# Hash attention followed by a PReLU feed-forward: GpSimd only adds exponentials, reciprocals spread by the block turn, ones product joined to the v product, one PSUM pool for both stages with two feed-forward groups to a tile

## The chip, the cores and the metric

One core of one Trainium2 chip. Times are device microseconds of one execution, and a kernel's time is the median of its runs. Runs that agree within a fraction of a per cent are called fast; a kernel that ran only once has a run of unknown state, which is said where it matters. The granted clock is the share of its full rate that TensorE was given, as the trace records it. PSUM is the memory that takes TensorE's outputs; it is divided into banks, and a tile is a buffer of one or more of them.

## The reference

Attention in which a query sees only the keys of its own hash bucket (6 sign bits of a projection), then a feed-forward layer with a PReLU, all in float32.

```
batch, n_heads, seq, head_dim = (4, 8, 768, 64)
n_tokens, d_model, d_ff = (3072, 512, 2048)

q_bits = (einsum('bhsd,dk->bhsk', q, proj) > 0)          # k_bits likewise
mask   = q_bucket[:, :, :, None] == k_bucket[:, :, None, :]
scores = where(mask, scale * matmul(q, k.T), -1e9)
attn   = exp(scores - max) / (sum(exp(scores - max)) + 1e-9)
x      = matmul(attn, v)       # (B,H,S,D) -> (B*S, H*D)

h = x @ w_in
g = maximum(h, 0) + alpha * minimum(h, 0)
out = g @ w_out
```

## The kernel before

Work is cut into 16 head pairs, each of two units of 384 queries; a period in this text is one pair. In the loop, unit u computes scores in three parts of two key blocks, and beside that the unit before it, u-1, is finished: its exponentials summed (`add_first` on GpSimd, `add_last` on VectorE), multiplied by v (`attend`), summed over the keys by a product with ones, and divided. In between stand turns (transposes) and hash products of the next pair, and the conversion of the weights. TensorE's outputs go to small PSUM tiles: two `sc` tiles of two banks each, two `av`, two `mi`. The last are shared by the turns, the hash products and the sums.

```
    for u in range(UNITS + 1):
        ...
        if live:
            scores(u, 0)
            add_first(u, 0)
        if u > 0:
            add_last(u - 1)
            attend(u - 1, 0)
        if more:
            if g == 0:
                turn(pi + 1, "q", 0)
                turn(pi + 1, "q", 1)
            else:
                hash_bits(pi + 1, 0)
        if live:
            weight_parts(u)
            weight_sum(u)             # GpSimd
            scores(u, 1)
            add_first(u, 1)
        if u > 0:
            attend(u - 1, 1)
            ...
        if more:
            if g == 0:
                turn(pi + 1, "k", 0)
                turn(pi + 1, "k", 1)
            else:
                hash_bits(pi + 1, 1)
        if live:
            scores(u, 2)
        if u > 0:
            divide(u - 1)             # begins with the product with ones
        if live:
            weight_sign(u)
            ...
    attn.close()                      # frees SBUF and PSUM of the attention

    mpool = ctx.enter_context(tc.tile_pool(name="mlp", bufs=2))
    mpsum = ctx.enter_context(tc.tile_pool(name="mps", bufs=4, space=bass.MemoryType.PSUM))

    def ff1(b, ch, f):
        ps = mpsum.tile([P, CW], F32, name=f"h{b}_{ch}_{f}", tag="h", bufs=4)
        ...                           # four matmuls of 128x128 by 128x384, two passes each
        do(DVE.tensor_scalar(neg, ps, 0.0, alpha[:, f : f + 1], op0=ALU.min, op1=ALU.mult))
        ...
        do(DVE.scalar_tensor_tensor(g, ps, 0.0, neg, op0=ALU.max, op1=ALU.add))
```

## Time and profile before

| | before |
|---|---|
| time | 1087.3 us, median of 4 runs (1086.52 to 1089.06) |
| profiled span | 1082.9 us, granted clock 0.996 |
| attention, to the end of the last score product | 399.6 us |
| from there to the start of the third group of h | 19.75 us |
| from there to the end | 663.5 us |

The prediction below shows the page and the waits.

After the first wait TensorE stands for only 2.1 us in the second stage, in the verdict (a check of the inputs' magnitudes). One period of the attention, by the windows view (length, then busy us and instructions of each engine, clock, DMA share, GB/s):

```profile
252.00:276.69 24.69, 23.59 (x160) 10.37 (x156) 20.21 (x32) 15.96 (x27) 13.25 (x8) 1.00 0.33 91
```

TensorE is busy for 23.59 of 24.69 us.

### The profile page before, as it was taken

Reading aid. Unit: us, or ns where it says so; the run is one execution under the profiler, and the core shown is the slowest. Engines: PE = TensorE matmul, PEld = TensorE weight load, DVE = VectorE, ACT = ScalarE, POOL = GpSimd, SP = SyncE. Lnnn points to the kernel's source line nnn. Section 1 sums busy time; section 2 is a strip of 40 time slices with the busy share of each in tenths; the row PEclk is TensorE's granted clock in tenths of the full one; section 3 lists DMA queues with packets and bytes.
Section 4 is the critical chain, followed back from the end, with each engine's and each line's share of the span. In section 5 each row is a group of like instructions: output and inputs, shape, how many; then the busy total and the mean of one; then the engine's idle time right before and its main releaser. Section 6 shows DMA issues by size and latency. Waiting matters only on the chain.

```text
span 1082.9 us, 10697 instructions
## 1 busy us (share of the span) xinstructions
PE 1042.6 (96%) x4292; PEld 508.9 (47%) x4292; DVE 483.8 (45%) x795; ACT 271.1 (25%) x441; POOL 214.8 (20%) x144
## 2 busy tenths in 40 slices
PE   6999999999999998999999999999999999999997
PEld 3444444444444434544544544544544544554543
DVE  4887888878888794401411410410410420420410
ACT  6566666666656640000000000000000000000000
POOL 4455555455544560000000000000000000000000
PEclk9999999999999998999999999999999999999999
DMA  6333333333333200000000000000000000000000
GB/s 172 92 83 84 84 93 103 88 98 83 98 87 99 69 1 1 1 10 20 0 10 19 1 10 20 1 10 20 1 10 20 0 10 19 1 10 14 6 10 22
DMA packets 62843, 42.73 MB, mean 39 GB/s; under 512 B 51504, under 2 KB 55616, under 8 KB 62784
## 3 DMA queue, kind: packets, MB, share of 16 engines
q1 hardware_dynamic: 62784, 41.96, 13.7%
q8 instruction: 35, 0.57, 0.2%
q14 instruction: 24, 0.20, 0.1%
HBM read 35.66 MB, written 6.29 MB: 39 GB/s over the span
## 4 chain that ended last, share of the span: by engine, by line
PE 78%; DVE 17%; ACT 3%; issue 1%; DMA 0%; SPq 0%; POOL 0%; DVEq 0%; ACTq 0%
PE h L735 31%; PE z L748 30%; PE sc L603 7%; PE av L635 6%; DVE st L658 2%; DVE kb L588 2%; DVE accd L624 2%; DVE accd L625 2%; ACT pt L608 1%; PE sm L651 1%; PE tp_k L567 1%; PE tp_q L567 1%; DVE wr L549 1%; ACT qb L591 1%; DVE xT L660 1%
## 5 line engine op out<-in xcount | busy, mean ns | idle before, releaser
L735 PE MATMUL h<-xT,w_in 128*128 128x384 f32 x1024 | 333.4, 488 | 2.9 <-DVE xT L660 2.9
L748 PE MATMUL z<-w_out,g 128*128 128x512 f32 x768 | 330.9, 592 | 0.0
L740 DVE TENSOR_SCALAR neg<-h,alpha 128x384 f32<-128x384 f32 x128 | 79.1, 618 | 467.3 <-PE h L735 467.3
L735 PEld LDWEIGHTS h<-xT,w_in 128*128 128x128 f32 x1024 | 195.2, 191 | 141.3 <-issue 8.6
L748 PEld LDWEIGHTS z<-w_out,g 128*128 128x128 f32 x768 | 145.9, 190 | 182.0 <-issue 179.9
L753 ACT COPY o<-z 128x512 f32<-128x512 f32 x24 | 14.0, 585 | 663.2 <-PE z L748 663.2
L603 PE MATMUL sc<-qT,kT 64*128 64x384 f32 x768 | 155.5, 482 | 0.0
L608 ACT ACTIVATE pt<-sc 128x768 f32<-128x768 f32 x192 | 148.4, 808 | 21.7 <-PE sc L603 20.9
L635 PE MATMUL av<-pt,vn 128*64 128x385 f32 (+1 forms) x768 | 137.9, 494 | 0.0
L619 POOL TENSOR_TENSOR accp<-accp,pt 128x768 f32<-128x768 f32 x64 | 108.5, 1695 | 2.5
L635 PEld LDWEIGHTS av<-pt,vn 128*64 128x64 f32 x768 | 49.6, 136 | 80.4 <-issue 80.4
L603 PE MATMUL sc<-qb,kb 64*128 64x384 bf16 x384 | 64.1, 326 | 16.9 <-ACT pt L608 16.8
L603 PEld LDWEIGHTS sc<-qT,kT 64*128 64x128 f32 x768 | 69.1, 188 | 14.7 <-issue 14.4
L742 DVE SCALAR_TENSOR_TENSOR g<-h,neg 128x384 f32<-128x384 f32 x128 | 71.4, 558 | 4.4
L616 POOL TENSOR_TENSOR accp<-pt,pt 128x768 f32<-128x768 f32 x32 | 64.5, 2016 | 39.4 <-ACT pt L608 38.6
L603 PEld LDWEIGHTS <-kb 64*128 64x128 bf16 x384 | 24.1, 93 | 77.3 <-issue 61.1
L591 ACT ACTIVATE qb<-hs,bq 32x384 bf16<-32x384 f32 x64 | 36.6, 573 | 79.4 <-DVE kb L588 78.8
L624 DVE TENSOR_TENSOR accd<-pt,pt 128x768 f32<-128x768 f32 x32 | 54.7, 1710 | 0.0
L658 DVE COPY st<-rc 128x384 f32<-128x384 f32 x32 | 46.3, 1446 | 1.1
L655 DVE STREAM_TRANSPOSE st<-sm 128x384 f32<-128x384 f32 x32 | 18.6, 582 | 54.7 <-PE sm L651 54.7
L552 POOL TENSOR_TENSOR wr<-w_out,wr 128x512 f32<-128x512 f32 x16 | 20.6, 1285 | 76.3 <-DVE vs L641 42.0
L552 POOL TENSOR_TENSOR wr<-w_in,wr 128x512 f32<-128x512 f32 x16 | 20.5, 1282 | 72.3 <-DVE vs L641 41.5
(73 smaller groups left out, 467.5 us busy)
## 6 DMA issues: line engine op xcount, KB each, us to landing
raw<-in_moe_w_in_dram SPq DMA_DIRECT2D x16, 512.0 KB, 3.8
raw<-in_moe_w_out_dram SPq DMA_DIRECT2D x16, 512.0 KB, 3.6
qn<-in_q_dram SPq DMA_DIRECT2D x32, 192.0 KB, 3.3
kn<-in_k_dram SPq DMA_DIRECT2D x32, 192.0 KB, 3.2
vn<-in_v_dram SPq DMA_DIRECT2D x16, 384.0 KB, 3.2
out_dram<-o SPq DMA_DIRECT2D x24, 256.0 KB, 2.0
wh<-in_proj_dram SPq DMA_DIRECT2D x2, 1.5 KB, 2.5
alpha<-in_moe_alpha_dram SPq DMA_DIRECT2D x1, 8.0 KB, 1.9
```

The lines of the kernel that those rows point to most:

```text
L591: do(ACT.activation(bits["q", pi][D * s : D * s + 32, cols], ps[r], AF.Sign, bias=bq[r]))
L603: do(PE.matmul(sc[:, s, :CW], what["k", pi][r, ks], what["q", pi][r, qs], start=first, stop=not first,))
L608: do(ACT.activation(pt[:, :, :CW], sc[:, :, :CW], AF.Exp, scale=SCALE))
L616: do(POOL.tensor_tensor(accp[u], p[0], p[1], op=ALU.add))
L619: do(POOL.tensor_tensor(accp[u], accp[u], t, op=ALU.add))
L624: do(DVE.tensor_tensor(accd[u], p[0], p[1], op=ALU.add))
L635: do(PE.matmul(av[u][D * s : D * s + D, :w], nat["v", pi][:, s, kc * D : (kc + 1) * D], prob[u, kc][:, s, :w], start=(kc == 0), stop=(kc = ...
L658: do(DVE.tensor_copy(a.rearrange("p (n w) -> p n w", w=32), r.unsqueeze(2).to_broadcast([P, CW // 32, 32])))
L735: do(PE.matmul(ps, w[:, kk, o : o + P], xT[b][:, kk, ch * CW : (ch + 1) * CW], start=(kk == 0), stop=(kk == NK - 1),))
L740: do(DVE.tensor_scalar(neg, ps, 0.0, alpha[:, f : f + 1], op0=ALU.min, op1=ALU.mult))
L742: do(DVE.scalar_tensor_tensor(g, ps, 0.0, neg, op0=ALU.max, op1=ALU.add))
L748: do(PE.matmul(ps, gT[b, ch, f][:, t * P : (t + 1) * P], w_out[f // 4][:, f % 4], start=(f == 0), stop=(f == NF - 1),))
```

## The change

The intent, as I read it: VectorE and GpSimd contend for SBUF ports in the attention (a copy of 0.36 us takes 1.65 beside GpSimd, in the prediction's lines), and TensorE stands between the two stages. So GpSimd keeps only the adds of exponentials (the weight sum goes to VectorE); the copy that spreads the reciprocals goes, and the second 32x32 block transpose reads a broadcast operand instead; the product with ones follows the product with v directly, so that the array changes its tiling less often; and one PSUM pool serves both stages, so that the first two groups of h can run inside the last chunk's tail. For the last part the groups of h take the two `sc` tiles, two groups to a tile of two banks.

```
     def weight_sum(i):
-        do(POOL.tensor_tensor(wr[i], piece(i)[0], wr[i], op=ALU.add))
-    def weight_sign(i):
         lo, hi = halves(i)
+        do(DVE.tensor_tensor(wr[i], piece(i)[0], wr[i], op=ALU.add))
         do(DVE.scalar_tensor_tensor(...))                    # sign
 ...
+    def totals(u):
+        sums[u] = psum.tile([P, CW], F32, name=f"sm{u}", tag="mi")
+        for s in range(2):
+            do(PE.matmul(sums[u][D * s : D * s + D], ones, accd[u][:, s], start=True, stop=True))
 ...                                                          # in divide:
-        do(DVE.tensor_copy(a.rearrange("p (n w) -> p n w", w=32), r.unsqueeze(2).to_broadcast([P, CW // 32, 32])))
-        do(DVE.transpose(d, a))
+        do(DVE.transpose(d, r.unsqueeze(2).to_broadcast([P, CW // 32, 32])))
 ...                                                          # the loop
+        weight_parts(u)
         if more: ... turn q / hash half 0
-        if live:
-            weight_parts(u)
-            weight_sum(u)
         scores(u, 1)
         add_first(u, 1)
+        weight_sum(u)
         if u > 0:
             attend(u - 1, 1)
+            totals(u - 1)
         if more: ... turn k / hash half 1
         scores(u, 2)
         if u > 0:
             divide(u - 1)
-            weight_sign(u)
 ...
     def ff1(b, ch, f):
-        ps = mpsum.tile([P, CW], F32, name=f"h{b}_{ch}_{f}", tag="h", bufs=4)
+        if f % 2 == 0:
+            hs[b, ch] = psum.tile([P, 2, 512], F32, name=f"h{b}_{ch}_{f}", tag="sc")
+        ps = hs[b, ch][:, f % 2, :CW]
 ...
+    attend(last, 0)
+    ff1(0, 0, 0)
+    add_last(last)
+    attend(last, 1)
+    ff1(0, 0, 1)
+    totals(last)
+    divide(last)
+    attn.close()
```

Cut: nine instead of eight exponential buffers, smaller pools, the output z in the `av` tiles, the verdict in the `mi` tiles.

More of the change, by code (lines that the diff above doesn't have):

```diff
@@ L432, in fast_path @@
     const = ctx.enter_context(tc.tile_pool(name="const", bufs=1))
+    first = ctx.enter_context(tc.tile_pool(name="first", bufs=2))
+    psum = ctx.enter_context(tc.tile_pool(name="ps", bufs=2, space=bass.MemoryType.PSUM))
     attn = ctx.enter_context(ExitStack())
     pool = attn.enter_context(tc.tile_pool(name="sb", bufs=2))
-    psum = attn.enter_context(tc.tile_pool(name="ps", bufs=2, space=bass.MemoryType.PSUM))
     pairs = [(b, hp) for b in range(B) for hp in range(NP)]
@@ L458, in fast_path @@
     xT = [const.tile([P, NP, S], F32, name=f"xT{b}") for b in range(B)]
-    NPT = 8
-    pts = [const.tile([P, 2, CW + 1], F32, name=f"pt{i}") for i in range(NPT)]
+    NPT = 9
+    pts = [pool.tile([P, 2, CW + 1], F32, name=f"pt{i}", bufs=1) for i in range(NPT)]
     n_pt = [0]
     nat, tr, bits = {}, {}, {}
-    prob, accp, accd, av, vsum = {}, {}, {}, {}, {}
+    prob, accp, accd, av, vsum, sums = {}, {}, {}, {}, {}, {}
     def load(pi, name):
@@ L622, in add_last @@
         p = [prob[u, NC - 2 + i][:, :, :CW] for i in range(2)]
-        accd[u] = pool.tile([P, 2, CW], F32, name=f"accd{u}", tag="accd")
+        accd[u] = pool.tile([P, 2, CW], F32, name=f"accd{u}", tag="accd", bufs=1)
         do(DVE.tensor_tensor(accd[u], p[0], p[1], op=ALU.add))
@@ L630, in attend @@
         if half == 0:
-            av[u] = psum.tile([P, CW + 1], F32, name=f"av{u}", tag="av")
+            av[u] = psum.tile([P, 512], F32, name=f"av{u}", tag="av")
         w = CW + 1 if g == 0 else CW
@@ L648, in divide @@
         b, hp = pairs[pi]
-        ps = psum.tile([P, CW], F32, name=f"sm{u}", tag="mi")
-        for s in range(2):
-            do(PE.matmul(ps[D * s : D * s + D], ones, accd[u][:, s], start=True, stop=True))
         a = pool.tile([P, CW], F32, name=f"st{u}", tag="st", bufs=1)
@@ L654, in divide @@
         d = pool.tile([P, CW], F32, name=f"dn{u}", tag="dn", bufs=1)
-        do(DVE.transpose(a, ps))
+        do(DVE.transpose(a, sums[u]))
         do(DVE.tensor_scalar(r, a.rearrange("p (n w) -> p n w", w=32)[:, :, 0], S * EPS, None, op0=ALU.add))
         do(DVE.reciprocal(r, r))
-        do(DVE.tensor_copy(a.rearrange("p (n w) -> p n w", w=32), r.unsqueeze(2).to_broadcast([P, CW // 32, 32])))
-        do(DVE.transpose(d, a))
+        do(DVE.transpose(d, r.unsqueeze(2).to_broadcast([P, CW // 32, 32])))
         do(DVE.scalar_tensor_tensor(
@@ L680, in fast_path @@
     weight_abs(0)
-    for u in range(UNITS + 1):
+    for u in range(UNITS):
         pi, g = divmod(u, NCH)
-        live, more = u < UNITS, pi + 1 < NPAIR and u < UNITS
-        if live:
-            scores(u, 0)
-            add_first(u, 0)
+        more = pi + 1 < NPAIR
+        scores(u, 0)
+        add_first(u, 0)
         if u > 0:
@@ L695, in fast_path @@
                 hash_bits(pi + 1, 0)
-        if live:
-            weight_parts(u)
-            weight_sum(u)
-            scores(u, 1)
-            add_first(u, 1)
+        scores(u, 1)
+        add_first(u, 1)
+        weight_sum(u)
         if u > 0:
             attend(u - 1, 1)
+            totals(u - 1)
             if g == 0 and 0 < pi < NPAIR - 1:
@@ L710, in fast_path @@
                 hash_bits(pi + 1, 1)
-        if live:
-            scores(u, 2)
+        scores(u, 2)
         if u > 0:
             divide(u - 1)
-        if live:
-            weight_sign(u)
-            load_weight(u + 3)
-            if u + 1 < NW:
-                weight_abs(u + 1)
+        load_weight(u + 3)
+        if u + 1 < NW:
+            weight_abs(u + 1)
         if more:
@@ L723, in fast_path @@
                 load(pi + 2, "qk"[g])
-    attn.close()
-    mpool = ctx.enter_context(tc.tile_pool(name="mlp", bufs=2))
-    mpsum = ctx.enter_context(tc.tile_pool(name="mps", bufs=4, space=bass.MemoryType.PSUM))
-    gT = {}
+    gT, hs = {}, {}
     def ff1(b, ch, f):
-        ps = mpsum.tile([P, CW], F32, name=f"h{b}_{ch}_{f}", tag="h", bufs=4)
+        if f % 2 == 0:
+            hs[b, ch] = psum.tile([P, 2, 512], F32, name=f"h{b}_{ch}_{f}", tag="sc")
+        ps = hs[b, ch][:, f % 2, :CW]
         w, o = w_in[f // (NF // 4)], (f % (NF // 4)) * P
@@ L738, in ff1 @@
             ))
-        neg = mpool.tile([P, CW], F32, name=f"neg{b}_{ch}_{f}", tag="neg")
+        early = b == ch == 0 and f < EARLY
+        neg = first.tile([P, CW], F32, name=f"neg{b}_{ch}_{f}", tag="neg")
         do(DVE.tensor_scalar(neg, ps, 0.0, alpha[:, f : f + 1], op0=ALU.min, op1=ALU.mult))
-        g = mpool.tile([P, CW], F32, name=f"g{b}_{ch}_{f}", tag="g", bufs=NF + 4)
+        where, bufs = (first, EARLY) if early else (mpool[0], NF + 2)
+        g = where.tile([P, CW], F32, name=f"g{b}_{ch}_{f}", tag="g", bufs=bufs)
         do(DVE.scalar_tensor_tensor(g, ps, 0.0, neg, op0=ALU.max, op1=ALU.add))
@@ L745, in ff2 @@
     def ff2(b, ch, t):
-        ps = mpsum.tile([P, DM], F32, name=f"z{b}_{ch}_{t}", tag="z", bufs=2)
+        ps = psum.tile([P, DM], F32, name=f"z{b}_{ch}_{t}", tag="av")
         for f in range(NF):
@@ L751, in ff2 @@
             ))
-        o = mpool.tile([P, DM], F32, name=f"o{b}_{ch}_{t}", tag="o")
+        o = mpool[0].tile([P, DM], F32, name=f"o{b}_{ch}_{t}", tag="o")
         do(ACT.copy(o, ps))
@@ L762, in verdict @@
         for n in range(3):
-            ps = mpsum.tile([1, P], F32, name=f"vd{n}", tag="vd", bufs=1)
+            ps = psum.tile([1, P], F32, name=f"vd{n}", tag="mi")
             do(PE.transpose(ps, top[:, n : n + 1], ident))
@@ L771, in verdict @@
         do(DVE.tensor_scalar(flag, row[:, 0:1], -1.0, 1.0, op0=ALU.mult, op1=ALU.add))
+    EARLY = 2
+    mpool = []
     chunks = [(b, ch) for b in range(B) for ch in range(NCH)]
-    EARLY = 2
+    last = UNITS - 1
+    attend(last, 0)
[6 more added lines that the diff above has]
+    attn.close()
+    mpool.append(ctx.enter_context(tc.tile_pool(name="mlp", bufs=2)))
     for n, (b, ch) in enumerate(chunks):
-        for f in range(EARLY if n else 0, NF):
+        for f in range(EARLY, NF):
             ff1(b, ch, f)
```

## The prediction

> **What bounds the kernel now.** I first read the page: busy time by engine and the slices.
>
> ```profile
> PE 1042.6 (96%) x4292; PEld 508.9 (47%) x4292; DVE 483.8 (45%) x795; ACT 271.1 (25%) x441; POOL 214.8 (20%) x144
> PE   6999999999999998999999999999999999999997
> DVE  4887888878888794401411410410410420420410
> POOL 4455555455544560000000000000000000000000
> ```
>
> There are two stages. To about 400 us the attention runs, with VectorE near 85% busy beside a TensorE at 95%; from 412 us the feed-forward part runs, where TensorE never waits and VectorE idles. The second stage is 128 groups h of eight matmuls (2.58 us each) and 24 z: 333.4 + 330.9 us of matmul. The change does not touch this work, so it can gain only before 415 us.
>
> Next, one period of the attention (one head pair, two units), 252.0 to 276.69 us: by the windows view TensorE is busy for 23.59 of 24.69 us, VectorE for 20.21, GpSimd for 13.25. The waits of that period (total us, times, longest):
>
> ```profile
> ACT qb L591 <- DVE kb L588: 5.2, 2, 5.0
> DVE st L655 <- PE sm L651: 3.7, 2, 1.9
> PE sc L603 <- ACT pt L608: 1.1, 2, 0.8
> ```
>
> TensorE loses 1.1 us per pair, all in front of score products that wait for exponentials to empty a PSUM buffer. VectorE has 3.7 us of slack, in front of the ones product. Why the exponentials are late shows in the timeline (start, duration, engine):
>
> ```profile
> 253.59 0.67 DVE L588 TENSOR_SCALAR kb<-hs,tk,mk 128x384 bf16<-128x384 f32 x1
> 254.29 1.16 ACT L591 ACTIVATE qb<-hs,bq 32x384 bf16<-32x384 f32 x2 [0.21 <-DVE kb L588]
> 255.48 1.51 ACT L608 ACTIVATE pt<-sc 128x768 f32<-128x768 f32 x2
> 256.34 0.34 PE L603 MATMUL sc<-qb,kb 64*128 64x384 bf16 x2 [0.32 <-ACT pt L608]
> ```
>
> This is a chain: hash product, kb on VectorE, qb on ScalarE, exponential, next unit's scores. It returns in the prediction.
>
> Last, VectorE against GpSimd, and the seam between the stages:
>
> ```profile
> 259.99 2.16 POOL L616 TENSOR_TENSOR accp<-pt,pt 128x768 f32<-128x768 f32 x1 [1.59 <-ACT pt L608]
> 260.40 2.57 DVE L624 TENSOR_TENSOR accd<-pt,pt 128x768 f32<-128x768 f32 x1
> ...
> 269.63 1.65 DVE L658 COPY st<-rc 128x384 f32<-128x384 f32 x1
> ...
> 408.49 1.18 PE L651 MATMUL sm<-accd,ones 128*64 128x384 f32 x4 [4.20 <-DVE accd L625]
> 410.79 0.36 DVE L658 COPY st<-rc 128x384 f32<-128x384 f32 x1
> 412.56 0.98 PE L735 MATMUL h<-xT,w_in 128*128 128x384 f32 x1 [2.90 <-DVE xT L660]
> ```
>
> The add takes 2.57 us here and 0.95 beside an idle GpSimd; it ends one bare add after GpSimd does. The copy takes 1.65 against 0.36. At the seam TensorE stands 4.2 and 2.9 us.
>
> **What the Trainium skill says.** (1) "SBUF — State Buffer", section "Who interferes with whom": a VectorE instruction with two SBUF inputs, or one in a 2-port mode, contends with a GpSimd instruction that reads SBUF, and the later one waits for the whole of the other. The trace agrees: 2.57 and 1.65 us above. It also shows the loser served at the next boundary: from 21 to 28 us the two engines take turns, one instruction each. (2) "PSUM — Partial Sum Buffer", section "PSUM bank collisions raise a hardware error": two engines may not read one bank and quadrant together. It agrees: qb waits 5.2 us per pair for kb, which reads the same tile. (3) "TensorE: Matmul & The Clock Gate", section "What's actually happening": an idle window of about 3.4 us halves the clock. It agrees: after the 4.2 us stand the windows view grants 0.50 from 410 to 414 us, and the first h group ends 4.43 instead of 2.58 us after its start. (4) "GPSIMD Engine Reference", section "Performance versus the Vector engine": a two-input add is 1.96 times slower on GpSimd. Here 1.70 against 0.95 us, 1.8 times.
>
> **Part by part.**
>
> Reciprocals by the block turn. The copy goes: 32 x 1.446 = 46.3 us of VectorE, some 35 of it waiting for GpSimd (0.36 is the bare time). The second transpose reads a broadcast instead; I keep it at 0.58.
>
> Weight sum to VectorE. GpSimd loses 1.28 us per unit; VectorE gets an add of 512 columns, by scaling the 0.95 us of 768 columns about 0.68. Bare VectorE work per unit changes by -0.36 + 0.68 = +0.3 us. But now three exponential adds (1.83 + 1.73 + 1.73 = 5.3 us) stand in the same stretch as four or five contending VectorE instructions in a row.
>
> Ones product behind the v product. A group of matmuls costs more than its stream whenever the array's tiling switches: av 2.09 us against 6 x 0.3225 = 1.94, sm 0.80 against 0.645, scores 1.72 against 1.61. Two groups fewer per unit save 0.155 + 0.105, so 0.5 per pair. The sum of all groups of a pair without waits is 23.45 us now, so the new floor is about 22.95. Against 24.69 that would be 1.7 us per pair.
>
> But the move has two costs. First, scores of a unit now follow the hash product with only one score group (1.61 us) between. The chain needs 0.05 + 0.67 + 0.05 + 1.16 + 0.05 + 0.76 + 0.05 = 2.8 us after the hash product: a TensorE bubble of about 1.1 us per pair, where 1.1 us of waits was before. Second, the sums now hold one of the two small PSUM tiles while the two key turns are issued. The second turn needs a buffer: either the one VectorE frees by its first transpose in divide, or the first turn's, which ScalarE frees (bubble 0.5).
>
> How late is VectorE? By hand, time 0 at a turn unit's first scores: the last exponential of the unit before ends at 0.8; two adds to 2.75; weight parts until GpSimd's first add begins at about 4.1. From there VectorE has 2.5 us of contending work and GpSimd 5.3, taking turns, so the transpose starts near 11.5. The sums are ready at 9.05. If the turn waits for that transpose, the bubble is about 2.6 us.
>
> The seam. Now: scores end at 399.55, h starts at 412.56 and loses 4.43 - 2.58 = 1.85 to the clock: 14.85 us. Then: av 4.17, last sums 0.8, a switch or two; the two early h groups fill the waits. That is 5.2. Gain 9.6 us, and the clock stays up. Verdict with two buffers: 0.5. The last pair, without turns: 0.5.
>
> **The rivals.** With 14.5 periods that have turns and hashes, and 10.6 us from seam, verdict and last pair:
>
> A. The turn waits for the sums' transpose. Pair 22.95 + 1.1 + 2.6 = 26.7 to 26.8 us, +2.1 each, +30: 1087.7 + 30 - 10.6 = 1107. For: two tiles only, strict alternation in the startup trace. Against: an author who reordered weight parts and hash bits so carefully would have seen it.
>
> B. The turn takes the other buffer, but VectorE becomes the bound: bare work 17 us, gaps 1.3, waiting for GpSimd up to 7 per pair, so 25.0 us, +0.3: 1081.
>
> C. VectorE is hindered less than I count (the copy, its worst victim, is gone, and GpSimd no longer waits for VectorE): 22.95 + 1.1 + 0.3 = 24.4, -0.3: 1073.
>
> D. The bubbles nearly vanish and TensorE's floor rules: 23.6 us, -1.1 or a little more, with 17 to 19 us gained besides the seam: 1059.
>
> **Range and chances.** The seam is the firm part, near -10 us or 0.9%. The periods decide the rest; their sign is open. I choose weights 0.28, 0.20, 0.30 and 0.22: 310 + 216 + 322 + 233 = about 1080 us. My hand schedule alone leans to A or B; I weight C and D up because it chains many small times, and the diff looks tuned. Faster by over 2% means below 1066, nearly only D plus the good end of C: 0.26. Slower by over 2% means above 1109, the bad end of A: 0.13. Range 1056 to 1109.
>
> **What would show it.** Right: no TensorE stand over 1 us near the seam and clock 1.00 there; the copy's row gone; one score wait of about 1 us per pair behind qb. The period tells A to D apart: 26.8, 25.0, 24.4, 23.6. In A the waits list has the key turn on the transpose of the sums, some 2 us each; in B VectorE has almost no idle time. Wrong: the feed-forward groups slower than 2.58 us (halves of one PSUM tile hindering each other), a transpose of a broadcast far over 0.58, or a seam that keeps a stand because VectorE arrives late with the last sums.

## More of the kernel before

In the feed-forward stage every group h has a PSUM tile of its own, one of four.

The costliest groups of instructions (line, engine, operation, count, then busy us and mean ns, then idle time ahead and its releaser):

```profile
L735 PE MATMUL h<-xT,w_in 128*128 128x384 f32 x1024 | 333.4, 488 | 2.9 <-DVE xT L660 2.9
L748 PE MATMUL z<-w_out,g 128*128 128x512 f32 x768 | 330.9, 592 | 0.0
L740 DVE TENSOR_SCALAR neg<-h,alpha 128x384 f32<-128x384 f32 x128 | 79.1, 618 | 467.3 <-PE h L735 467.3
```

## The result, and the profile after

| | before | after |
|---|---|---|
| time | 1087.3 us (1086.52 to 1089.06, 4 runs) | 1210.4 us (1209.45 to 1211.87, 4 runs) |
| profiled span | 1082.9 us | 1208.9 us |
| to the end of the last score product | 399.6 us | 436.7 us |
| from there to the start of the third group of h | 19.75 us | 10.45 us |
| from there to the end | 663.5 us | 761.7 us |

The changed kernel is slower: ratio 1.1131, 95% interval 1.1112 to 1.1150. A ratio here is the mean time of one kernel's fast runs over that of the other's of the same rounds, so it is not quite the ratio of the medians quoted. The profiled run of the kernel before was 2.6 us quicker than its median, so differences of spans are that much larger than differences of medians.

The spans differ by 126.0 us, and the table splits it: +37.1 in the attention, -9.3 at the seam, +98.2 in the feed-forward stage, where the prediction expected nothing. I looked there first. The costliest groups again, after:

```profile
L730 PE MATMUL h<-xT,w_in 128*128 128x384 f32 x1024 | 349.2, 493 | 82.0 <-DVE g L739 82.0
L745 PE MATMUL z<-w_out,g 128*128 128x512 f32 x768 | 330.9, 592 | 0.0
L736 DVE TENSOR_SCALAR neg<-h,alpha 128x384 f32<-128x384 f32 x128 | 79.0, 618 | 561.6 <-PE h L730 561.5
```

z is what it was. TensorE's idle time ahead of h went from 2.9 to 82.0 us, and what ended it is g, the second half of the PReLU on VectorE. At the same time VectorE waits for h, 561.5 us instead of 467.3. Two engines that wait for each other, neither of them busy: that is a handshake, not a shortage. The list of waits after (engine, line, releaser: total us, times, longest) gives its count:

```profile
PE h L730 <- DVE g L739: 82.0, 63, 1.3
```

63 waits of 1.30 us for 128 groups: one group in two. The timeline shows which (start, duration, engine, line, operation, idle time before it and its releaser):

```profile
548.67 5.43 PE L730 MATMUL h<-xT,w_in 128*128 128x384 f32 x16 [1.30 <-DVE g L739]
551.56 0.62 DVE L736 TENSOR_SCALAR neg<-h,alpha 128x384 f32<-128x384 f32 x1 [2.94 <-PE h L730]
552.21 0.56 DVE L739 SCALAR_TENSOR_TENSOR g<-h,neg 128x384 f32<-128x384 f32 x1
554.14 0.62 DVE L736 TENSOR_SCALAR neg<-h,alpha 128x384 f32<-128x384 f32 x1 [1.37 <-PE h L730]
554.79 0.56 DVE L739 SCALAR_TENSOR_TENSOR g<-h,neg 128x384 f32<-128x384 f32 x1
555.41 0.91 PE L730 MATMUL h<-xT,w_in 128*128 128x384 f32 x2 [1.30 <-DVE g L739]
```

The block of 16 matmuls at 548.67 is two groups of eight: first the second half of one tile, then, without a wait, the first half of the other tile. Then TensorE waits until VectorE has read that first half (neg and g, 0.62 + 0.56 us and the gaps), and only then begins the second half of the same tile, which nobody reads. Two groups take 555.41 - 548.67 = 6.74 us instead of 2 x 2.58 = 5.16. The trace records the semaphores that an instruction waits for: the first matmul of all 64 second halves carries a wait on VectorE, and in 61 of the 64 first halves it carries none. So the wait was put there when the program was built: a write into a tile after a read of that tile, although the read was of the other half. Of the 98.2 us, 82.0 are waits, and 15.8 are h's own busy time (349.2 - 333.4), 0.25 us each time the array starts again.

The attention: one period after, by the windows view, and the waits that TensorE had in it:

```profile
236.00:262.85 26.85, 23.51 (x156) 10.45 (x156) 23.18 (x31) 16.07 (x26) 10.95 (x6) 1.00 0.30 84
```

```profile
PE tp_k L566 <- DVE st L656: 2.1, 1, 2.1
PE sc L602 <- ACT pt L607: 1.3, 2, 1.1
```

A period takes 2.16 us more than before. TensorE's busy time is nearly what it was, its idle time three times as long, VectorE 3 us busier. The larger wait is in front of the second key turn (tp_k), which needs a small PSUM tile that VectorE frees by transposing the sums (st). The timeline before it:

```profile
257.87 3.92 POOL L618 TENSOR_TENSOR accp<-accp,pt 128x768 f32<-128x768 f32 x2 [1.19 <-ACT pt L607]
258.20 2.06 DVE L554 TENSOR_TENSOR wr<-w_out,wr 128x512 f32<-128x512 f32 x1
259.53 0.81 PE L646 MATMUL sm<-accd,ones 128*64 128x384 f32 x4
260.29 2.05 DVE L555 SCALAR_TENSOR_TENSOR w_out<-raw,wr 128x512 uint32<-128x512 uint32 x1
262.26 0.57 DVE L656 STREAM_TRANSPOSE st<-sm 128x384 f32<-128x384 f32 x1
262.89 0.55 PE L566 MATMUL tp_k<-ident,kn 128*128 128x128 f32 x3 [2.07 <-DVE st L656]
```

The sums are ready at 260.3. VectorE has the weight sum and the sign first, and each shares its stretch with one of GpSimd's two adds: 2.06 and 2.05 us, where beside an idle GpSimd each takes 0.69 (at 437.14 and 437.87 us of the same trace). The transpose starts 2 us late, and the turn with it.

The 14 periods with this wait account for 14 x 2.16 = 30.2 of the 37.1 us. Another 6.4 come from the clock: in four periods the stand before the second key turn was followed by half speed, and they took 28.4 to 28.5 us each. One of them, by the windows view (the clock is the third value from the end):

```profile
206.00:208.00 2.00, 0.45 (x3) 0.38 (x3) 1.90 (x5) 0.00 (x0) 0.45 (x1) 0.93 0.03 2
208.00:210.00 2.00, 2.00 (x10) 0.95 (x10) 1.19 (x2) 0.48 (x1) 0.00 (x0) 0.50 0.81 264
```

At the seam the change does what it was made for: early h groups fill the waits, and the clock stays at 1.00.

```profile
440.00:444.00 4.00, 4.00 (x18) 1.65 (x18) 3.05 (x6) 0.00 (x0) 0.00 (x0) 1.00 0.00 0
444.00:448.00 4.00, 4.00 (x15) 1.89 (x14) 2.24 (x4) 0.00 (x0) 0.00 (x0) 1.00 0.00 0
```

### The profile page after: what moved, and what is told of

Same layout as the page of the kernel before. It is cut to its first block, busy times and chain, and to the rows that moved or that the text cites. A ratio compares the mean times of both kernels' runs of the same rounds, so it can differ in the third digit from the quotient of the medians.

```text
span 1208.9 us, 10709 instructions
## 1 busy us (share of the span) xinstructions
PE 1063.4 (88%) x4292; PEld 507.0 (42%) x4292; DVE 525.0 (43%) x795; ACT 272.5 (23%) x441; POOL 178.5 (15%) x113
## 4 chain that ended last, share of the span: by engine, by line
PE 71%; DVE 24%; ACT 2%; issue 1%; DMA 1%; SPq 0%; DVEq 0%; ACTq 0%
PE h L730 29%; PE z L745 27%; PE sc L602 6%; PE av L634 5%; DVE neg L736 3%; DVE g L739 3%; DVE wr L554 2%; PE hs L586 2%; DVE rc L657 2%; DVE accd L624 1%; DVE accd L623 1%; ACT pt L607 1%; DVE w_out L555 1%; DVE st L656 1%; DMA qn<-in_q_dram 1%
## 5 line engine op out<-in xcount | busy, mean ns | idle before, releaser
L730 PE MATMUL h<-xT,w_in 128*128 128x384 f32 x1024 | 349.2, 493 | 82.0 <-DVE g L739 82.0
L736 DVE TENSOR_SCALAR neg<-h,alpha 128x384 f32<-128x384 f32 x128 | 79.0, 618 | 561.6 <-PE h L730 561.5
L730 PEld LDWEIGHTS h<-xT,w_in 128*128 128x128 f32 x1024 | 189.0, 190 | 242.0 <-DVE g L739 120.8
L602 PE MATMUL sc<-qT,kT 64*128 64x384 f32 x768 | 159.8, 494 | 0.0
L618 POOL TENSOR_TENSOR accp<-accp,pt 128x768 f32<-128x768 f32 x64 | 116.3, 1817 | 79.5 <-ACT pt L607 76.9
L615 POOL TENSOR_TENSOR accp<-pt,pt 128x768 f32<-128x768 f32 x32 | 59.9, 1872 | 177.0 <-ACT pt L607 177.0
L602 PE MATMUL sc<-qb,kb 64*128 64x384 bf16 x384 | 65.5, 334 | 19.2 <-ACT pt L607 19.1
L566 PE MATMUL tp_k<-ident,kn 128*128 128x128 f32 x96 | 18.9, 315 | 29.3 <-DVE st L656 27.1
L623 DVE TENSOR_TENSOR accd<-pt,pt 128x768 f32<-128x768 f32 x32 | 31.9, 997 | 27.3 <-ACT pt L607 27.3
L624 DVE TENSOR_TENSOR accd<-accd,accp 128x768 f32<-128x768 f32 x32 | 33.8, 1056 | 3.7 <-DVE accd L623 0.5
L587 DVE TENSOR_SCALAR kb<-hs,tk,mk 128x384 bf16<-128x384 f32 x32 | 21.6, 675 | 22.8 <-PE hs L586 22.8
L567 ACT COPY kT<-tp_k 128x384 f32<-128x384 f32 x32 | 15.3, 483 | 63.7 <-PE tp_k L566 63.7
```

The source lines that it names most:

```text
L602: do(PE.matmul(sc[:, s, :CW], what["k", pi][r, ks], what["q", pi][r, qs], start=first, stop=not first,))
L615: do(POOL.tensor_tensor(accp[u], p[0], p[1], op=ALU.add))
L618: do(POOL.tensor_tensor(accp[u], accp[u], t, op=ALU.add))
L623: do(DVE.tensor_tensor(accd[u], p[0], p[1], op=ALU.add))
L624: do(DVE.tensor_tensor(accd[u], accd[u], accp[u], op=ALU.add))
L730: do(PE.matmul(ps, w[:, kk, o : o + P], xT[b][:, kk, ch * CW : (ch + 1) * CW], start=(kk == 0), stop=(kk == NK - 1),))
```

## The experiments

Two theories stood at first. T1: the two-group tile makes the loss of the second stage, because the tool that builds the program tracks dependencies by tile and takes a tile as one object. Its rival: something that the trace puts in the same place, such as where z now lies in PSUM, or a contention of banks. For the attention, T2: the key turn waits for a small PSUM tile that VectorE frees late, because GpSimd's adds and the weight sum stand before the transpose; rival: the new order itself costs it. All kernels gave the right output except one, which is said there. The kernel before was run beside them and had medians of 1087.4 to 1088.2 us. The last experiment ran on another chip than the rest, where the kernel before took 1088.2.

### Own tile for each group (e1_own_tile)

```
-        if f % 2 == 0:
-            hs[b, ch] = psum.tile([P, 2, 512], F32, name=f"h{b}_{ch}_{f}", tag="sc")
-        ps = hs[b, ch][:, f % 2, :CW]
+        hs[b, ch] = psum.tile([P, 2, 512], F32, name=f"h{b}_{ch}_{f}", tag="sc")
+        ps = hs[b, ch][:, 0, :CW]
```

> The changed kernel, but each feed-forward group h has a two-bank PSUM tile of its own and uses one half. Theory 1 (the odd group waits because VectorE still reads the other half of its tile): the 63 waits of 1.30 us and the refill of about 0.27 us behind each go, 63 x 1.57 = 99 us, so about 1112 us, and the h groups follow each other every 2.58 us. Rival (the merged pool itself, or the smaller number of g buffers, slows the feed-forward part): it stays above 1190 us. Attention stays at 26.85 us per pair in both.

Measured: 1110.95 us (1110.33 to 1112.62), ratio to before 1.0218 (1.0198 to 1.0238): 99.4 us less than the changed kernel, though h now has only two buffers instead of four halves. Its row:

```profile
L729 PE MATMUL h<-xT,w_in 128*128 128x384 f32 x1024 | 332.4, 486 | 0.0
```

No wait, and z still lies where the change put it. So z's place is not the cause.

### The kernel before with two groups to a tile (e2_half_tiles)

```
-        ps = mpsum.tile([P, CW], F32, name=f"h{b}_{ch}_{f}", tag="h", bufs=4)
+        if f % 2 == 0:
+            hs[b, ch] = mpsum.tile([P, 2, 512], F32, name=f"h{b}_{ch}_{f}", tag="h", bufs=2)
+        ps = hs[b, ch][:, f % 2, :CW]
```

> The kernel before, with only its h groups put two to a tile, as halves. Theory 1: 64 waits of about 1.3 us plus refill appear, about 1087 + 99 = 1186 us, attention unchanged at 24.69 us per pair. Rival (the waits come from the pool shared with the attention): 1087 us.

Measured: 1189.57 us (one run, state unknown), 102.1 over the kernel before. The wait:

```profile
PE h L739 <- DVE g L746: 83.3, 64, 1.3
```

This one edit makes the whole loss: 83.3 us of waits and 19.2 of h's busy time (352.6 against 333.4).

### Both groups' matmuls before either PReLU (e3_pair_order)

The two groups keep their shared tile; only the program order changes, so that no write into it comes after a read of it.

```
+        if f % 2 == 1:
+            prelu(b, ch, f - 1)
+            prelu(b, ch, f)
+
+    def prelu(b, ch, f):
+        ps = hs[b, ch][:, f % 2, :CW]
```

> The changed kernel with two h groups per tile, but the matmuls of both are issued before either is read by VectorE. Theory 1a (the wait is put on a matmul that writes a tile after VectorE has begun to read it): no write follows a read inside a tile, so the waits go, about 1112 us as with own tiles. Rival 1b (two neighbouring banks of one tile hinder each other whatever the order): stays near 1210 us. Small cost allowed: the two readings come together.

Measured: 1112.23 us (one run, state unknown), and no wait of TensorE on h:

```profile
L730 PE MATMUL h<-xT,w_in 128*128 128x384 f32 x1024 | 332.4, 486 | 0.0
```

Same tiles, same banks, no loss: it is the order of write after read, inside one tile. With this T1 is settled.

### The seam alone (e4_seam_only)

The kernel before, in its own loop order, with one PSUM pool (and the other pools as the change has them), own tiles for h, and the early groups:

```
+    attend(last, 0)
+    ff1(0, 0, 0)
+    add_last(last)
+    attend(last, 1)
+    ff1(0, 0, 1)
+    totals(last)
+    divide(last)
```

> The attention loop of the kernel before, with the one PSUM pool and the early h groups (own tiles). Theory: only the seam gains, 9.4 us as read from the two traces (20.0 us before against 10.6), clock 1.00 there, so 1078 us. Rival (the seam gain is paid back because h groups hold the scores' buffers): 1085 us or more.

Measured: 1077.55 us (1076.64 to 1077.93), ratio 0.9906 (0.9889 to 0.9924), and TensorE fully busy at clock 1.00 across the seam. This part is a gain of 9.9 us by itself, by the medians.

### GpSimd's adds made small (e5_small_adds)

e1_own_tile with the adds of exponentials cut to 16 columns per head. Its output is wrong, which doesn't matter for the time.

```
-                do(POOL.tensor_tensor(accp[u], accp[u], t, op=ALU.add))
+                do(POOL.tensor_tensor(accp[u][:, :, :16], accp[u][:, :, :16], t[:, :, :16], op=ALU.add))
```

> e1_own_tile with GpSimd's three adds per unit cut from 768 to 32 columns (16 per head); the sums and so the output are wrong on purpose. Theory 2 (VectorE is late for the transpose of the sums because it takes turns with GpSimd's adds): the second key turn waits 0.3 us instead of 2.1, the clock dips go, the period falls from 26.85 to about 24.4 us, time about 1070 us; the wait behind qb of 1.1 us per pair stays. Rival (VectorE's own added work makes it late): the key turn still waits over 1 us, about 1100 us.

Measured: 1080.92 us (one run, state unknown), 30.0 less than e1_own_tile. The wait before the key turn in e1_own_tile, then the waits here:

```profile
PE tp_k L566 <- DVE st L656: 27.1, 14, 2.1
```

```profile
PE sc L603 <- ACT pt L608: 19.1, 30, 1.1
...
PE tp_k L567 <- DVE st L657: 2.9, 14, 0.2
```

The wait before the key turn falls from 27.1 to 2.9 us, the clock dips are gone, and the period is 24.99 us. So GpSimd's turns do delay the transpose. But I expected 24.4 a period and about 1070: without that wait the new order is still no quicker than the old one, because the score waits remain and what TensorE has to do was not 22.95 us.

### The weight sum back on GpSimd (e6_sum_on_gpsimd)

```
     def weight_sum(i):
+        do(POOL.tensor_tensor(wr[i], piece(i)[0], wr[i], op=ALU.add))
+
+    def weight_sign(i):
 ...
-        do(DVE.tensor_tensor(wr[i], piece(i)[0], wr[i], op=ALU.add))
 ...
+        weight_sum(u)
         scores(u, 1)
         add_first(u, 1)
-        weight_sum(u)
 ...
             divide(u - 1)
+        weight_sign(u)
```

> e1_own_tile with the weight sum on GpSimd again and the sign after divide, as before; all else as changed. Theory 2: two contending VectorE instructions fewer stand ahead of the transpose of the sums, by the hand schedule VectorE then waits for the sums and not the sums for it: key turn waits about 0.3 us, period about 24.4 us, near 1072 us. Rival (it is the joined ones product alone that costs): the key turn still waits about 2 us, near 1110 us.

Measured: 1082.0 us (1081.29 to 1082.1), ratio 0.9949 (0.9932 to 0.9966); the period is 24.99, and the wait before the key turn:

```profile
PE tp_k L568 <- DVE st L658: 2.9, 14, 0.2
```

The same as with small adds, with a right output: it is enough that the weight sum and the sign don't stand before the transpose. The direction was right, the size 10 us off for the reason given above.

### The ones product back before the division (e7_ones_before_divide)

```
             attend(u - 1, 1)
-            totals(u - 1)
 ...
         if u > 0:
+            totals(u - 1)
             divide(u - 1)
```

> e1_own_tile with the ones product back behind the scores, just ahead of divide. Theory 2: no PSUM tile is held over the key turns, so no key turn waits; the wait behind qb falls to about 0.3 us; but the two regroupings (0.5 us per pair) are lost and VectorE has 25 us of work and turns with GpSimd per pair: period near 25 us, about 1080 us. Rival (VectorE alone bounds the pair whatever the order): period stays 26.5 us or more, about 1108 us.

Measured: 1084.65 us (1082.88 to 1085.13), ratio 0.9968 (0.9949 to 0.9987). The key turn no longer waits, since no sums hold a tile then, but one wait of scores of 1.5 to 2.0 us a pair stands instead (22.9 us in 15), where I expected 0.3. A period is 25.2 us.

These three say: the joined ones product is what puts the key turn behind VectorE, but taking it back gains no more than taking away the delay does.

### The second half of turns and hash after the last scores (e8_late_half)

e1_own_tile with one block moved. The transpose of the sums then comes ahead of the turn that needs their tile, in program order as well as in time, and qb, which waits for kb, stands on ScalarE behind the exponentials of the last scores and no longer ahead of them. That half of the hash is not needed before the second score group of a later unit.

```
+        scores(u, 2)
+        if u > 0:
+            divide(u - 1)
         if more:
             if g == 0:
                 turn(pi + 1, "k", 0)
                 turn(pi + 1, "k", 1)
             else:
                 hash_bits(pi + 1, 1)
-        scores(u, 2)
-        if u > 0:
-            divide(u - 1)
```

> e1_own_tile with the second key turn pair and the second hash half issued after the last scores and divide instead of ahead of them. Theory 2 and the chain through qb: both TensorE waits lose their cause (the key turns come 1.7 us later, after the sums are due to be read; exponentials no longer queue behind the second qb). If TensorE then rules, the period is 23.5 us and the time about 1062 us; if VectorE with its turns rules, near 25 us and 1082 us. If the waits were caused by something else, they stay, near 1110 us.

Measured: 1063.96 us (1063.4 to 1064.54), ratio 0.9783 (0.9765 to 0.98). The period and the only waits of TensorE that recur:

```profile
200.00:223.78 23.78, 23.22 (x160) 10.36 (x156) 19.92 (x32) 15.80 (x27) 11.78 (x7) 1.00 0.33 95
```

```profile
PE sc L602 <- ACT pt L607: 10.6, 18, 1.4
```

No wait before the key turn, no dip (clock 0.999), half the score waits. This is the fastest version that I found, better than both kernels.

### The broadcast transpose alone (e9_broadcast_turn)

e4_seam_only with the copy taken out:

```
-        do(DVE.tensor_copy(a.rearrange("p (n w) -> p n w", w=32), r.unsqueeze(2).to_broadcast([P, CW // 32, 32])))
-        do(DVE.transpose(d, a))
+        do(DVE.transpose(d, r.unsqueeze(2).to_broadcast([P, CW // 32, 32])))
```

> e4_seam_only with only the reciprocals' copy replaced by the transpose of a broadcast. Theory 3 (the copy, mostly a wait for GpSimd, delays kb and so the exponentials): the transpose stays at 0.58 us, the two score waits of 0.8 and 0.3 us per pair shrink to about 0.3 together, 14.5 x 0.8 = 12 us, so about 1066 us. Rival (the next two-input instruction takes the copy's place in the queue with GpSimd): 1075 to 1078 us.

Measured: 1066.99 us (1066.37 to 1069.85), ratio 0.9809 (0.9792 to 0.9826), 10.6 less than e4_seam_only. The score waits, first e4_seam_only, then this kernel:

```profile
PE sc L604 <- ACT pt L609: 16.9, 29, 1.1
```

```profile
PE sc L604 <- ACT pt L609: 11.2, 28, 0.5
```

They fall by 5.7 us (I expected 0.3 a pair to remain; it is 0.9 in a window). The period goes from 24.8 to 24.44 us, which is about 5 us in all. In the traces the last score product ends 7.6 us earlier (394.0 against 401.6 us) and the spans differ by 7.8: about the 5.7 of waits and 2.4 of TensorE's busy time (1043.0 to 1040.6). The other 2.8 of the 10.6 can't be seen there, because the profiled run of this kernel, with 1069.85 us, was 2.9 slower than its median.

### The late half without the rest of the change (e10_late_half_alone)

e4_seam_only, with its copy, its GpSimd weight sum and its separate ones product, and e8's move:

```
+        scores(u, 2)
+        if u > 0:
+            totals(u - 1)
+            divide(u - 1)
         if more: ... turn k / hash half 1
-        scores(u, 2)
-        if u > 0:
-            totals(u - 1)
-            divide(u - 1)
```

> e4_seam_only with the second key turn pair and hash half issued after the last scores and divide; copy, sum on GpSimd and separate ones product as in the kernel before. If the order of this one piece is what e8_late_half gained, the score waits go and the floor of the separate groups rules: 23.5 to 23.8 us per pair, about 1062 us. If the regrouping and the moved sum matter as well, it stays above 1068 us.

Measured: 1117.15 us (1115.19 to 1118.62), ratio 1.0273 (1.025 to 1.0297): wrong by 55 us. The waits, VectorE's and TensorE's:

```profile
DVE st L658 <- PE sm L648: 130.9, 31, 6.9
```

```profile
PE sc L604 <- ACT pt L609: 29.3, 18, 3.0
```

Here the ones product comes after the last scores, so the transpose waits for it (130.9 us, against 54.3 in e4_seam_only). Its division, with a copy of 1.46 us, is then still running when the hash product is ready, and kb behind it comes late; qb, the exponentials and the next scores follow, some of these at half clock. In e8_late_half the sums are ready before the last scores begin. So the move does not work without the rest of the change. The place of the weight sum is not what it needs (e11_late_half_sum_on_gpsimd below); whether it is the joined ones product alone, as the waits suggest, or the missing copy as well, no run separates.

### The late half with the weight sum on GpSimd (e11_late_half_sum_on_gpsimd)

e8_late_half, with the edit of e6_sum_on_gpsimd.

> e8_late_half with the weight sum on GpSimd and the sign after the late half, as before. VectorE has 0.7 us less per unit, GpSimd 1.28 more. Theory: in e8_late_half VectorE still waits for TensorE somewhere in each pair (about 2 us), so it is not the bound; moving the sum changes little, 1062 to 1066 us. Rival (VectorE's lateness makes the remaining 0.6 us score wait): about 1056 us.

Measured: 1066.81 us (1066.39 to 1067.02), ratio 0.9808 (0.9791 to 0.9825); the period is about 23.9. Once the transpose doesn't release a turn, the place of the weight sum is worth 3 us, in favour of VectorE.

### Squares after the next scores (e12_squares_after_scores)

e8_late_half, with ScalarE's weight magnitude and sum of squares moved behind the next unit's first two exponentials, to take away the score wait that is left:

```
         scores(u, 0)
+        if u > 0:
+            weight_abs(u)
+            if was_more:
+                magnitude(was_pi + 1, "qk"[was_g])
+                ...                           # the load of a later q or k moves along
 ...
-        if u + 1 < NW:
-            weight_abs(u + 1)
-        if more:
-            magnitude(pi + 1, "qk"[g])
-            ...                               # and its load
```

> e8_late_half with ScalarE's weight magnitude and sum of squares (0.7 + 1.0 us per unit) issued after the next unit's first two exponentials instead of ahead of them. Theory: the last score wait, 0.56 us per pair, is there because those exponentials queue behind the two; it goes, and 15 x 0.6 = 8 us with it, about 1056 us. Rival: GpSimd's first add now starts 1.7 us earlier and meets VectorE's two adds of the probabilities, VectorE falls behind by a turn (1.7 us) and the wait comes back elsewhere, 1062 us or more.

Measured: 1068.84 us (1068.56 to 1069.04), ratio 0.9822 (0.9806 to 0.9838). The waits:

```profile
PE tp_k L566 <- DVE st L656: 11.2, 14, 0.9
...
PE sc L602 <- ACT pt L607: 2.2, 3, 1.8
```

The score wait is gone, as meant, and the wait before the key turn is back, as the rival said. One wait was exchanged for another, and the time is 4.9 us over e8_late_half.

## Why the prediction was right or wrong

**The step that failed** is the sentence "The change does not touch this work, so it can gain only before 415 us". It was read from what the matmuls do, and those are the same. But the change moves the outputs of h from four tiles to halves of two, and a half is not a tile: 63 waits of 1.30 us and the restarts behind them, 98 us. e2_half_tiles makes the loss out of the kernel before with that edit alone, e1_own_tile and e3_pair_order take it out of the changed kernel. The prediction named the layout only in its last paragraph, under "Wrong", as "halves of one PSUM tile hindering each other", and gave it no size. It could have had one: by the groups of the kernel before, two PReLU instructions take 0.62 and 0.56 us; once for every two groups, 64 times, that is 75 us before any gap.

**The seam** was right: -9.6 expected, -9.3 in the trace, -9.9 in e4_seam_only by the medians, clock 1.00. One term was 0.2 too large: from start to start the first h group took 4.23 us (412.56 to 416.79) and so lost 1.65, not 1.85; the 4.43 runs to 416.99, where VectorE begins to read it.

**The rival A** was right as a mechanism and in its sum: pair 26.7 to 26.8 expected, 26.85 found; turn behind the transpose of the sums, 2.6 expected and 2.1 found; scores behind qb 1.1 expected, and 1.3 found in two waits, the longer one 1.1. With own tiles for h the kernel takes 1110.95 us where A said 1107. Yet two terms were off and made up for each other. The floor of 22.95 was too low: with about 1.5 us of waits left (19.1 us of scores over 14.5 pairs, and 0.2 before the key turn), e5_small_adds and e6_sum_on_gpsimd have periods of 24.99, so about 23.5 without waits, and TensorE's busy time after is 23.51, 0.08 below that of before instead of 0.5. Only in e8_late_half, without the long stands, is it 23.22. The other term, the delay of the transpose, was 0.5 too high.

The timeline shows which part of the 0.5 us that the regrouping was to save failed. From start to start, the product with v and the ones product behind it take 1.99 + 0.74 us after, against 2.09 + 0.80 before: the 0.155 per unit came. But the two score groups that now follow each other take 3.62 us or more in all 31 cases, each with a wait, where two groups apart took 2 x 1.72. In e8_late_half a turn or a hash product stands between them again.

**The weights** were wrong. My own schedule pointed to A, and I gave it 0.28, because the author "would have seen it"; the weighted mean was 1080, and own tiles alone give 1110.95. e5_small_adds and e6_sum_on_gpsimd show the cause that the schedule had: what VectorE does between the sums and the transpose, at GpSimd's pace.

**Not foreseen**: four clock dips in the attention, 6.4 us.

**The copy** was right: its row is gone and the broadcast transpose takes 0.578 us. By itself it is worth 10.6 us by the medians and 7.8 by the traces (e9_broadcast_turn). In the changed kernel that gain can't be seen, because, as I read it and no run shows by itself, the key turn's wait covers it.

So without the shared tile the change costs 2.2%; with the shared tile 11.3%; with own tiles and one block moved it gains 2.2% (e8_late_half). The difference of 23.8 us there is, in the traces, 9.3 us at the seam, 11.0 in the attention (the last score product ends at 388.6 instead of 399.6 us) and 0.5 behind it. That is 20.8, and 2.6 more comes from the quick profiled run of the kernel before.

One reading in the prediction was loose. The 5.2 us of qb's wait for kb are ScalarE's idle time. Of the longest stand, from 246.37 to 251.39 us, 1.7 us passed before the hash product was done at 248.06, and kb itself began only at 250.68, behind other work of VectorE. So these 5.2 us do not measure what reading the same tile costs.

## What to carry to other kernels

When PSUM pools are merged, look at every tile that is written in parts and read in between: whoever tracks dependencies by tile will put a wait between the halves, and one dependency of a microsecond, repeated at every second group, was here worth more than all else in the change. Where a small buffer is held by a result, count what the engine that frees it does first, at the pace that contention gives it, and ask whether the work that needs the buffer can be issued after the release. And when your own schedule of the waits and your trust in the author disagree, believe the schedule.

## What the Trainium skill lacked or had wrong

- "PSUM — Partial Sum Buffer", section "Summary: rules for kernel authors", advises a different bank for reading while a matmul runs. The halves of the shared tile are two banks, and the program still waited, 63 times 1.30 us, because, as these runs show it, it was built with dependencies by tile. No page of those that I read says so. No run here writes one half while the other is read; with separate tiles (e1_own_tile) TensorE wrote one while VectorE read the other, and h lost nothing.
- "TensorE: Matmul & The Clock Gate", section "What's actually happening": it gives an idle window of about 3.4 us for the fall to half clock, and calls the window free-running. Here stands of about 2.1 us before the key turn were followed by a granted clock of 0.50 in 4 of 14 periods. The trace after fits a free-running window: its slow stretches in the attention begin at 98.49, 207.72, 289.64 and 398.87 us, whole multiples of 3.413 us apart, and last 3.41 us each. But the stretch of 3.41 us ahead of each was not idle: TensorE was busy for 1.33 to 1.45 us of it. After 1.62 and 1.64 us (from 368.15 and 177.00 us) the clock stayed full. How idle a window has to be, no run settles.
- No page that I found gives the cost of a block transpose that reads a broadcast operand: 578 ns for 128x384, the same as of a plain one before the change.
